# Six loads of keys and values move to a later place in a fused attention and expert kernel

## The chip, the cores and the metric

The kernel runs on one core of a Trainium2 chip. The time is the device time of one execution in microseconds; the figure for a kernel is the median of its runs. A core has TensorE (PE in the profile; its weight loads are PEld), VectorE (DVE), ScalarE (ACT), GpSimd (POOL) and SyncE (SP), and 16 DMA engines that serve the queues on which POOL and SP issue transfers.

## The reference

Keys and values are averaged over groups of 8 positions, softmax attention is done with the queries, and the context goes through four experts, whose outputs are added with per-token weights.

```
B, H, S, D = 8, 8, 576, 64                      # x: (4608, 512); 4 experts, hidden 1024
k_p, v_p = mean of k, v over groups of 8        # 72 pooled positions per head
attn = softmax(q @ k_p.T / sqrt(D)) @ v_p       # per batch and head
x = attn.transpose(0, 2, 1, 3).reshape(B * S, H * D)
for e in range(4):
    out += p[:, e:e + 1] * (relu(x @ w1[e]) @ w2[e])   # p: domain_probs normalised over e
```

## The kernel before

**Tiles and steps.** The 4608 tokens are 36 tiles of 128; four tiles are a group of 512. A batch has 576 tokens, so it covers four and a half tiles. The experts run in 36 steps (9 groups by 4 experts), each of 12 slots. In every three slots TensorE does two up-projections (`up`, L453, four matmuls each, for the next step) and one down-projection (`down`, L486, eight matmuls, for this step). That stream is the frame; all attention work for a later group is put between its slots.

**The plan.** `at(slot, fn, ...)` files a call under a slot, and the last loop emits, for each slot, the expert work first and then the calls filed there. Nothing is reordered afterwards: each engine runs its instructions in the order in which they were emitted. For tile t of groups 2 to 8, `base = (E * g - 5 + i) * SLOTS`, so tile 8 has base 36, tile 9 has 48, and so on by 12. `plan_tile` (L527) puts the scores (`sc`, L320) at slot base, the transposing DMA of the softmax weights (`attnT`, L390, SP) at base + 1, and the context (`x_ps`, L410) at base + 6. Directly behind the context it puts the transposing DMA of `x_sb` into `xT` (L430, SP), a `gate` on POOL and the load of the queries of tile t + 3 (`qrow`, L108, POOL).

**The gate.** `gate(t)` (L525) is a one-element POOL copy that reads `x_sb` of tile t. All that POOL issues behind it, loads included, therefore waits for the context of that tile.

**Keys and values.** A batch's raw keys and values are loaded by POOL with a cast to bf16 into `kraw` and `vraw` (L80 and L84: 512 and 64 KB each), two buffers of each. When a tile t begins a batch that was not prepared yet, `plan_batch` (L519) files, ahead of that tile, `prep_k` (DVE sums and mask, giving `kpad`) at base - 9, `prep_kT` at base - 6 and `prep_v` at base - 5. For batches 2 to 7 `prep_kT` is one transposing DMA on SP, `kT<-kpad` (L259). The first `sc` of the batch needs it at slot base, six slots later. Batch 2 begins with tile 9; batches 3, 4, 5, 6 and 7 are first needed by tiles 13, 18, 22, 27 and 31.

**The loads in question.** `waiting` is a list that starts with the loads of batch 3 and gets those of batch b + 2 when batch b is planned. In each pass over a tile, one load is taken from the list and filed at base + 6, so on POOL it stands behind the gate and the query load of that tile:

```
done_batches, waiting = 2, [(load_k, 3), (load_v, 3)]
...
    plan_tile(t, base - 2, -9 if t > 2 * TPG else 0)
    if waiting:
        load, b = waiting.pop(0)
        at(base + 6, load, b)
```

Slot base + 6 of tile t is slot (base of t + 1) - 6. So where tile t + 1 begins a batch, its `kT<-kpad` is filed at the same slot as a load that the pass over tile t files. In the kernel before this is so for tile 8 (batch 2, slot 42) and for no other tile, since the list is empty in the passes over tiles 12, 17, 21, 26 and 30.

Of the kernel before, what the change touches and what calls it, by code (L numbers as in the profile page):

```python
# [17 lines left out]
def kernel(  # L18
# [12 lines left out]
    B, H, S, D = q.shape  # L31
    E, DM, F = moe_w1.shape
    P = nc.NUM_PARTITIONS
# [481 lines left out]
    def at(slot, fn, *args):  # L515
        plan.setdefault(slot, []).append((fn, args))

    def plan_batch(b, slot):
        at(slot + 5, prep_k, b)  # L519
        at(slot + 8, prep_kT, b)  # L520
        at(slot + 9, prep_v, b)
# [5 lines left out]
    def plan_tile(t, slot, turn=0):  # L527
        exp, norm, move, sum_v = (3, 4, 3, 8) if by_dma(t) else (4, 5, 8, 10)
        at(slot + turn, turn_q, t)
        at(slot + 2, scores, t)  # L530
        at(slot + 2, less_max, t)
        at(slot + exp, expo, t)
        at(slot + move, attn_T, t)
        at(slot + norm, sums if by_dma(t) else normalise, t)
        at(slot + sum_v, context, t)
        if by_dma(t):
            at(slot + sum_v, gate, t)
            if t + 3 < NT:
                at(slot + sum_v, load_q, t + 3)
# [7 lines left out]
    done_batches, waiting = 2, [(load_k, 3), (load_v, 3)]  # L547
    for g in range(2, NG):
        for i in range(TPG):
            t = g * TPG + i  # L550
            base = (E * g - 5 + i) * SLOTS
            last_b = ((t + 1) * P - 1) // S
            if last_b >= done_batches:
                plan_batch(last_b, base - 2 - SLOTS)
                done_batches += 1
                if last_b + 2 < B:
                    waiting += [(load_k, last_b + 2), (load_v, last_b + 2)]
            plan_tile(t, base - 2, -9 if t > 2 * TPG else 0)
            if waiting:
                load, b = waiting.pop(0)  # L560
                at(base + 6, load, b)

# [198 lines left out]
```

## Time and profile before

| | us |
|---|---|
| median of 3 runs | 555.86 |
| lowest and highest of them | 554.24, 556.35 |
| the profiled execution, its own time | 556.4 |
| its span in the profile | 554.4 |
| TensorE busy in the span | 542.0 (98%) |
| `h_ps` L453 and `o_ps` L486 together | 547.5, of which each overlaps the next |
| POOL busy | 70.6 (13%) |

The last row but one is longer than TensorE's whole busy time because matmuls are pipelined: one begins before the one ahead of it has ended. Start times, not the durations of single matmuls, tell how long a stretch takes. "Landing" of a DMA is the time from its issue to the moment its last byte is signalled.

### The profile page before, as it was taken

The page shows a single profiled execution, that of the slowest core. Times are in us where ns is not written, and L with a number is a line of the kernel's source. Part 1 is how long each engine was busy: PE and PEld are TensorE (multiplying, and loading weights), DVE is VectorE, ACT ScalarE, POOL GpSimd, SP SyncE. Part 2 cuts the span into 40 slices and gives each one's busy share as a digit, 9 for nine tenths or more (in the row PEclk, how much of TensorE's full clock was granted, in tenths as well). Part 3 has the DMA queues.
Part 4 walks back from the last instruction along what each step waited for, and adds up shares of the span by engine and source line. Part 5 has one row for each costly group of instructions (what it writes and reads, how often), then busy time and mean ns, then how long its engine had stood idle before and what let it go on. Part 6 is the DMA issues. An engine that isn't in the chain of part 4 may idle for free.

```text
span 554.4 us, 7323 instructions
## 1 busy us (share of the span) xinstructions
PE 542.0 (98%) x2929; PEld 261.3 (47%) x2929; DVE 264.7 (48%) x456; ACT 213.5 (39%) x355; POOL 70.6 (13%) x120
## 2 busy tenths in 40 slices
PE   7899998999999999999999999999999999999997
PEld 3664553444444444444444444444444444444443
DVE  4874846344644445644463444744474444422223
ACT  3554653233333333333333333333333333333330
POOL 7234002111101100112011100101010000000000
PEclk9999999899999999999999999999999999999999
DMA  9999918455745534366535553334333431111002
GB/s 200 206 200 200 199 8 137 74 80 79 122 82 83 84 59 99 53 84 74 116 48 77 84 116 41 52 41 98 60 54 40 74 74 32 21 39 38 1 0 77
DMA packets 110689, 45.84 MB, mean 83 GB/s; under 512 B 87584, under 2 KB 106016, under 8 KB 110656
## 3 DMA queue, kind: packets, MB, share of 16 engines
q0 software_dynamic: 51472, 22.03, 32.3%
q1 hardware_dynamic: 59184, 23.35, 17.8%
q8 instruction: 23, 0.38, 0.3%
q14 instruction: 10, 0.08, 0.0%
HBM read 45.16 MB, written 9.44 MB: 98 GB/s over the span
## 4 chain that ended last, share of the span: by engine, by line
PE 93%; DMA 3%; DVE 2%; ACT 1%; issue 0%; POOL 0%; SPq 0%; POOLq 0%
PE o_ps L486 44%; PE h_ps L453 43%; PE x_ps L410 2%; PE sc L320 2%; DMA kT<-kpad 1%; PE h_ps L469 1%; DMA kraw<-in_k_dram 1%; PE x_ps L436 1%; PE o_ps L571 0%; DVE acc L501 0%; PE at_ps L394 0%; ACT attnT L395 0%; PE qT_ps L310 0%; DVE kraw L235 0%; DVE vraw L235 0%
## 5 line engine op out<-in xcount | busy, mean ns | idle before, releaser
L457 ACT ACTIVATE h_sb<-h_ps 128x512 bf16<-128x512 f32 x280 | 167.2, 597 | 301.3 <-PE h_ps L453 301.1
L453 PE MATMUL h_ps<-xT,w 128*128 128x512 bf16 x1120 | 275.2, 380 | 0.0
L486 PE MATMUL o_ps<-w,h_sb 128*128 128x512 bf16 x1152 | 272.3, 379 | 0.0
L486 PEld LDWEIGHTS <-h_sb 128*128 128x128 bf16 x1152 | 112.5, 98 | 134.5 <-issue 1.1
L501 DVE SCALAR_TENSOR_TENSOR acc<-o_ps,p_sb,acc 128x512 f32<-128x512 f32 x108 | 81.0, 750 | 180.4 <-PE o_ps L486 180.4
L453 PEld LDWEIGHTS <-w 128*128 128x128 bf16 x1120 | 106.1, 98 | 117.2 <-issue 0.6
L497 DVE TENSOR_SCALAR acc<-o_ps,p_sb 128x512 f32<-128x512 f32 x36 | 27.0, 750 | 62.1 <-PE o_ps L486 62.1
L525 POOL COPY gated<-x_sb 1x1 bf16<-1x1 bf16 x28 | 7.8, 278 | 372.2 <-DVE x_sb L416 372.2
L334 DVE TENSOR_REDUCE mx<-sc 128x8 f32<-128x576 f32 x36 | 27.2, 756 | 14.1 <-PE sc L320 14.1
L108 POOL DMA_DIRECT2D qrow<-in_q_dram x36 | 30.5, 850 | 26.3 <-DMA w<-in_moe_w_dram 15.2
L338 DVE TENSOR_TENSOR d_sb<-sc,mx 128x576 f32<-128x576 f32 x36 | 27.3, 757 | 1.2
L416 DVE SCALAR_TENSOR_TENSOR x_sb<-x_ps,rs 128x512 bf16<-128x512 f32 x29 | 20.1, 692 | 12.5 <-PE x_ps L410 12.1
L351 ACT ACTIVATE attn<-d_sb 128x576 bf16<-128x576 f32 x29 | 19.8, 682 | 3.6 <-DVE d_sb L338 0.5
L372 DVE TENSOR_REDUCE es<-attn 128x8 f32<-128x576 bf16 x28 | 20.8, 744 | 0.0
L320 PE MATMUL sc<-kT,qT 128*128 128x144 bf16 (+1 forms) x160 | 15.3, 229 | 3.1 <-DMA kT<-kpad 2.9
L320 PEld LDWEIGHTS <-qT 128*128 128x128 bf16 (+1 forms) x160 | 11.2, 101 | 11.5 <-issue 5.5
L410 PEld LDWEIGHTS <-attnT 128*128 128x128 bf16 (+1 forms) x160 | 12.2, 100 | 7.3 <-issue 1.3
L410 PE MATMUL x_ps<-vbd,attnT 128*128 128x192 bf16 (+5 forms) x160 | 14.7, 231 | 0.0
L571 PE MATMUL o_ps<-still 128*128 128x512 bf16 x38 | 11.8, 436 | 1.3 <-DVE still L144 1.3
L235 DVE TENSOR_TENSOR vraw<-vraw 128x1280 bf16<-128x1280 bf16 (+1 forms) x14 | 9.2, 654 | 0.2
L235 DVE TENSOR_TENSOR kraw<-kraw 128x1280 bf16<-128x1280 bf16 (+1 forms) x14 | 9.0, 640 | 0.2
L469 PE MATMUL h_ps<-xT,w 128*128 128x128 bf16 x128 | 7.8, 219 | 0.7 <-ACT xT L442 0.4
(76 smaller groups left out, 148.9 us busy)
## 6 DMA issues: line engine op xcount, KB each, us to landing
out_dram<-acc SPq DMA_DIRECT2D x36, 256.0 KB, 2.0
vraw<-in_v_dram POOLq DMA_DIRECT2D x8, 512.0 KB, 7.6
w<-in_moe_w_dram POOLq DMA_DIRECT2D x8, 512.0 KB, 16.1
w<-in_moe_w_dram POOLq DMA_DIRECT2D x4, 1024.0 KB, 16.2
kraw<-in_k_dram POOLq DMA_DIRECT2D x7, 512.0 KB, 7.3
qrow<-in_q_dram POOLq DMA_DIRECT2D x28, 128.0 KB, 3.8
qg<-in_q_dram SPq DMA_DIRECT2D x1, 1024.0 KB, 5.7
kraw<-in_k_dram POOLq DMA_DIRECT2D x2, 256.0 KB, 6.7
```

The costliest lines, as they stand in the source:

```text
L108: nc.gpsimd.dma_start(out=qrow[t][at:at + n], in_=q[b][:, tok:tok + n, :].rearrange("h p d -> p h d"),)
L320: nc.tensor.matmul(sc[at:at + n, pair // 2, (pair % 2) * PW:(pair % 2 + 1) * PW], lhsT=qT[t][:, pair, at:at + n], rhs=kT[b][:].rearrange(" ...
L334: nc.vector.reduce_max(out=mxs[t][:], in_=by_head(t), axis=AX.X)
L338: nc.vector.tensor_tensor(out=st[t][:], in0=by_head(t), in1=mxs[t][:].unsqueeze(3).to_broadcast([P, 2, 4, SP]), op=ALU.subtract,)
L372: nc.vector.reduce_sum(out=es[:], in_=e, axis=AX.X)
L410: nc.tensor.matmul(ps[at:at + n, h0 * D:(h0 + c1 - c0) * D], lhsT=attnT[t][:, i, at:at + n], rhs=flat[:, c0 * D:c1 * D], start=(i == 0), s ...
L416: nc.vector.scalar_tensor_tensor(out=x_sb[:].rearrange("p (h d) -> p h d", d=D), in0=ps[:].rearrange("p (h d) -> p h d", d=D), scalar=V_ME ...
L453: nc.tensor.matmul(ps[:], lhsT=w1_sb[e][:, kc, fb * P:(fb + 1) * P], rhs=xT[g][:, kc, :], start=(kc == 0), stop=(kc == KC - 1),)
L457: nc.scalar.activation(out=hs[s][:, fb, :], in_=ps[:], func=ACT.Relu)
L486: nc.tensor.matmul(ps[:], lhsT=hs[s][:, fb, i * P:(i + 1) * P], rhs=w2_sb[e][:, fb, :], start=(fb == 0), stop=(fb == FB - 1),)
L497: nc.vector.tensor_scalar_mul(out=accs[t][:], in0=ps[:], scalar1=p_sb[:, e, t:t + 1])
L501: nc.vector.scalar_tensor_tensor(out=accs[t][:], in0=ps[:], scalar=p_sb[:, e, t:t + 1], in1=accs[t][:], op0=ALU.mult, op1=ALU.add,)
```

## The change

A load is taken from the list only in passes in which the tile after this one begins no batch that is still to be planned. In a pass where it does, the load stays at the head of the list for the next pass.

```
             plan_tile(t, base - 2, -9 if t > 2 * TPG else 0)
-            if waiting:
+
+            if waiting and ((t + 2) * P - 1) // S < done_batches:
                 load, b = waiting.pop(0)
                 at(base + 6, load, b)
```

Worked through for all tiles, this moves six loads and leaves four; the number in each cell is the tile whose gate the load stands behind:

| load | k3 | v3 | k4 | v4 | k5 | v5 | k6 | v6 | k7 | v7 |
|---|---|---|---|---|---|---|---|---|---|---|
| before | 8 | 9 | 10 | 11 | 13 | 14 | 18 | 19 | 22 | 23 |
| after | 9 | 10 | 11 | 13 | 14 | 15 | 18 | 19 | 22 | 23 |

Taken by places: the place behind tile 8 no longer has a load, the place behind tile 15 gets one, and the other places keep one, of keys where it was of values and the other way round. No instruction is added or taken away, and only POOL's order changes; the orders of PE, DVE, ACT and SP are the same.

## The prediction

> **What bounds the kernel now.** I read the busy shares first, then TensorE's waits behind the start-up, the chain of work that ended last, and the order in time around the one wait. The page's shares and its clock row:
>
> ```profile
> PE 542.0 (98%) x2929; PEld 261.3 (47%) x2929; DVE 264.7 (48%) x456; ACT 213.5 (39%) x355; POOL 70.6 (13%) x120
> ...
> PEclk9999999899999999999999999999999999999999
> ```
>
> TensorE is busy for 542.0 of 554.4 us: 12.4 us of idleness is all there is. In the clock row one slice, the eighth (97 to 111 us), is below full speed. Of the list of waits from 60 us to the end, this is the only line in which a PE matmul waited:
>
> ```profile
> PE sc L320 <- DMA kT<-kpad: 2.9, 1, 2.9
> ```
>
> So behind the start-up, which the change doesn't touch, TensorE stands once, for 2.9 us. The chain of waits has the same transfer as its only DMA there:
>
> ```profile
> 89.62 7.65 DMA kT<-kpad
> ```
>
> The order in time around it, four engines of it:
>
> ```profile
> 89.07 0.88 POOL L108 DMA_DIRECT2D qrow<-in_q_dram  x1
> 89.62 1.28 SPq L259 DMA_TRANSPOSE kT<-kpad  x1
> ...
> 89.94 0.76 POOL L80 DMA_DIRECT2D kraw<-in_k_dram  x1
> ...
> 91.45 3.36 SPq L509 DMA_DIRECT2D out_dram<-acc  x2
> ...
> 93.50 1.03 PE L453 MATMUL h_ps<-xT,w 128*128 128x512 bf16 x4
> ...
> 97.41 0.64 PE L320 MATMUL sc<-kT,qT 128*128 128x144 bf16 x4 [2.88 <-DMA kT<-kpad]
> ```
>
> The keys of batch 2 are turned from 89.62 on, the raw keys of batch 3 start to load 0.3 us later, and the turned keys land at 97.27 (89.62 + 7.65). The first scores of tile 9 start at 97.41. Four `h_ps` matmuls stand ahead of them from 93.50; undisturbed, four take 0.86 us (from 112.43 to 113.29 in the next step), so the scores could have begun at 94.36.
>
> **The whole price of the stall** is more than the wait. The stretches of one microsecond (columns: busy of PE, PEld, DVE, ACT, POOL, then the granted clock):
>
> ```profile
> 96.00:97.00 1.00, 0.00 (x0) 0.00 (x0) 0.00 (x0) 0.00 (x0) 0.00 (x0) 1.00 1.18 256
> 97.00:98.00 1.00, 0.59 (x5) 0.61 (x6) 0.00 (x0) 0.00 (x0) 0.00 (x0) 0.53 1.18 270
> 98.00:99.00 1.00, 1.00 (x4) 0.29 (x2) 0.88 (x2) 0.00 (x0) 0.00 (x0) 0.50 0.64 195
> 99.00:100.00 1.00, 1.00 (x4) 0.32 (x3) 0.63 (x1) 0.21 (x1) 0.00 (x0) 0.50 0.04 16
> 100.00:101.00 1.00, 1.00 (x5) 0.46 (x4) 0.00 (x0) 0.96 (x2) 0.00 (x0) 0.77 0.00 0
> ```
>
> The granted clock falls to half at about 97.1 and is back at about 100.5, so the first work after the wait runs at half speed. The price comes from like places in two steps: the run of eight `h_ps` matmuls in the slots 39 and 40 starts at 82.81, that of slots 51 and 52 at 101.74, that of slots 63 and 64 at 116.13. The step with the stall takes 18.93 us, the next one, with the same work, 14.39. The stall costs 4.54: 2.88 of wait and 1.66 of slow clock.
>
> **What goes.** The change takes `load_k(3)` from behind tile 8, so nothing of 576 KB starts beside this transpose. How soon would it land then? The other five `kT<-kpad` of the same trace have no load of keys or values beside them. The answers by window give 4.3, 4.1, 3.7, 4.0 and 4.5 us to landing, against 7.7 here. All five have a query load beside them, as this one keeps (in four it is issued 0.5 to 0.8 us ahead, as here). The one of 4.3, at 151.80, also has two output stores issued 1.83 us behind it, just as here (91.45 - 89.62 = 1.83). So neither explains the 7.7; the raw keys do. By the slowest of the five it lands at 89.62 + 4.5 = 94.12; with 0.14 from landing to the matmul (97.27 to 97.41) the scores can start at 94.26, and TensorE gets to them at 94.36. The wait goes whole, with 0.1 us to spare by the slowest row and 0.5 by the median (4.1). No idle piece is then left to slow the clock. Gain: 4.54, of which I take 4.5.
>
> What is late next? The scores of tile 9 also need `qT` of tile 9, issued at 84.78 with 2.4 us to landing: no. Behind them, the softmax up to the issue of `attnT` takes 2.74 us in an undisturbed tile (113.29 to 116.03), its landing 2.6; the context comes about 7.2 us behind the scores (28 matmuls at 0.216 plus 0.25, then four more): 1.8 us of slack, and no PE wait is listed there for any tile.
>
> **What moves.** Each load costs POOL 0.76 + 0.56 = 1.3 us of issue; POOL then waits 11 to 13 us for the next gate, so nothing queues behind it. SP, the other queue, keeps its order. Costed at nothing, with cover:
>
> - Six loads come later. A step of 12 slots is 14.39 us, a slot 1.2. The tightest are v3, filed at slot 66 and folded at slot 91, and k3, at 54 and 87: 30 and 40 us, against a landing of at most 8.9 for any such load here. Their buffers were read long before (v5 at slot 126 follows the fold of v3 at 91). If this cover went, DVE and the next `kT` would be late; 20 us are in the way.
> - The places behind tiles 9, 10, 11, 13 and 14 have a load before and after, of the same size. Nothing changes there.
> - The place behind tile 15 is new: about 195.8, beside `xT` of tile 15, issued at 194.29. The first matmul of the next group needs it at 199.35, 5.06 us later. Trace rows with a load in the same place: 3.1 (tile 9), 3.3 (tile 10), 2.5 (tile 11), 3.2 (tile 19); without one 2.5. So 1.8 us of slack remain at the worst row. Below nothing isn't possible: no matmul waits there now. From above: stretched as `kT` was (7.65 - 4.1 = 3.55), it lands in 6.05, a wait of 1.0. I take nothing, by the four rows in that very place. `attnT` of tile 16, at 202.96, may meet the end of the load (at most 195.8 + 8.9 = 204.7); the slowest landing of any `attnT` is 3.5, and its context is at 207.37: 0.9 to spare.
>
> **The sum.** The profiled execution took 556.4 (span 554.4, 2.0 around it). 556.4 - 4.54 = 551.9, span 549.9. That execution lies 0.5 above the median of the runs, 555.86; on the median's footing 555.86 - 4.5 = 551.4, which I give.
>
> **A rule against part of it.** The row: the clock fell to half some 2.6 us into an idle piece of 2.9 us. The Trainium skill, "TensorE: Matmul & The Clock Gate", in "The HAM clock gate (the "warmup" mystery)", has the clock fall after at least one idle window of about 3.4 us, from windows that run freely. By that rule a 2.9 us gap should cost its length alone, 556.4 - 2.88 = 553.5; by the row it is 551.9. The same section's 3.4 us until full speed returns agrees with the row's 97.1 to 100.5. I go by the row for this execution. Whether every run pays the 1.66 the trace can't say; the lowest run shown, 554.24, is 1.62 under the median, about that sum, which is an estimate from two rows and no proof.
>
> **Rivals.**
>
> 1. *The transpose is still late, by less.* For: 0.1 us is all that the slowest row leaves. Against: the median row leaves 0.5. At a landing of 6 us, midway between the 4.5 and the 7.65, the wait is 1.4; the clock, which fell 2.6 us into the gap, stays. 551.4 + 1.4 = 552.8. 8%.
> 2. *The change doesn't do what it says:* something else made this transpose slow (it is the first of its kind by this path, and it stands behind the stores of 86.09), so the stall stays: 555.9. Against: the row at 151.80 has the same stores on both sides (147.39 and 153.63) and 4.3. 5%.
> 3. *Slower: the load behind tile 15 holds up `xT` of tile 15* until it is through itself. The place is the first `h_ps` of the next group at 199.35. By the slowest load, 8.9, it would end at 204.7: a wait of 5.3 and a slow clock of 1.66, together 7.0, less the 4.5 gained: 558.4. It decides from a landing of 9.6 us on (5.06 + 4.54), or 7.9 with the slow clock. Against: 2.5 to 3.3 in four rows of this very place. 2%.
>
> **Numbers.** Forecast 551.4 at 85%, rivals 8, 5 and 2. From 554.24 - 4.54 = 549.7, the fastest run with the whole price off, to 556.4 - 2.88 = 553.5, the slowest with the wait alone gone; that takes in the forecast and the first rival, and leaves out 7% and the rare. About 0.5% (2.8 us) is what a measurement of this kernel can tell from no change. Faster by more: the forecast and half of the first rival, taken down a little for runs that never paid the slow clock: 0.87. Within: 0.09. Slower: 0.04, the third rival and what I haven't seen.
>
> **What would show it.** Right: no PE wait on `kT<-kpad` behind the start-up; its landing near 4.1; the clock row at 9 in the eighth slice; 14.4 us from the slots 39 and 40 to 51 and 52; `xT` of tile 15 within 3.3. Wrong: a wait of `h_ps` L453 near 195 us on `xT`, or a landing over 4.7 of this `kT` without the raw keys beside it.

## The result, and the profile after

| | before | after |
|---|---|---|
| median, us (6 runs each) | 555.10 | 551.94 |
| lowest and highest | 554.23, 556.35 | 551.66, 552.01 |
| ratio, 95% interval | | 0.994 (0.9923 to 0.9957) |
| profiled execution, its span | 554.4 | 549.9 |

The kernel is faster by 3.2 us. The six runs after lie within 0.35 us. Those before lie in two groups, three at 554.2 to 554.3 and three at 555.9 to 556.4, and why they do is taken up with the run of that kernel again. Three single executions in the experiments took 665.74, 958.99 and 2564.28 us, far over all others of their kernels, and are left out of every median, ratio and range below.

The page of the changed kernel, its shares and its clock row:

```profile
PE 537.4 (98%) x2873; PEld 260.8 (47%) x2929; DVE 264.7 (48%) x456; ACT 213.5 (39%) x355; POOL 70.7 (13%) x120
...
PEclk9999999999999999999999999999999999999999
```

The eighth slice of the clock row is back at 9. (The trace has 2873 of PE's 2929 matmuls; some records are missing, so PE's busy time isn't compared.) In the list of waits from 60 us on no PE matmul waits for anything any more. The order in time at the same place:

```profile
89.12 0.88 POOL L108 DMA_DIRECT2D qrow<-in_q_dram  x1
89.67 1.28 SPq L259 DMA_TRANSPOSE kT<-kpad  x1
...
91.50 3.36 SPq L509 DMA_DIRECT2D out_dram<-acc  x2
...
93.55 1.03 PE L453 MATMUL h_ps<-xT,w 128*128 128x512 bf16 x4
...
94.41 0.41 PE L320 MATMUL sc<-kT,qT 128*128 128x144 bf16 x4
```

The scores start 0.86 us behind the four up-projections ahead of them, and carry no bracket with a wait. The DMA issues from 88 to 99 us have what was 7.7 before (last column: us to landing):

```profile
kT<-kpad SPq DMA_TRANSPOSE x1, 4.0
```

The step from the slots 39 and 40 (82.86) to 51 and 52 (97.25) takes 14.39 us, as every step does.

### The profile page after: what moved, and what is told of

Read it like the earlier page. It is cut to its first block, busy times and chain, and to the rows that moved or that the text cites. A ratio compares the mean times of both kernels' runs of the same rounds, so it can differ in the third digit from the quotient of the medians.

```text
span 549.9 us, 7267 instructions
## 1 busy us (share of the span) xinstructions
PE 537.4 (98%) x2873; PEld 260.8 (47%) x2929; DVE 264.7 (48%) x456; ACT 213.5 (39%) x355; POOL 70.7 (13%) x120
## 4 chain that ended last, share of the span: by engine, by line
PE 96%; DMA 1%; DVE 1%; issue 1%; ACT 1%; POOL 0%; POOLq 0%
PE o_ps L486 45%; PE h_ps L453 44%; PE x_ps L410 2%; PE sc L320 2%; PE h_ps L469 1%; DMA kraw<-in_k_dram 1%; PE x_ps L436 1%; PE o_ps L572 0%; PE at_ps L394 0%; ACT attnT L395 0%; PE qT_ps L310 0%; POOL kraw L80 0%; DVE mx L334 0%; DVE d_sb L338 0%; DVE acc L501 0%
## 5 line engine op out<-in xcount | busy, mean ns | idle before, releaser
L453 PE MATMUL h_ps<-xT,w 128*128 128x512 bf16 x1088 | 271.8, 379 | 1.5
```

What stands on the lines that cost most here:

```text
L453: nc.tensor.matmul(ps[:], lhsT=w1_sb[e][:, kc, fb * P:(fb + 1) * P], rhs=xT[g][:, kc, :], start=(kc == 0), stop=(kc == KC - 1),)
```

## The experiments

Theory A is that of the prediction: the load of keys beside the transpose is the whole cause. Its rivals are B, that the later places of the other loads bring a part, and, per experiment, that something else at this place makes the transpose slow. Theory C, that a part of the runs doesn't pay the slow clock, is to explain the two groups and with them the 3.2 us in place of 4.5. Theory D came later, from a miss.

The kernels start from the kernel before. Except for that kernel run again and the last experiment, they give the places of the loads outright, in this form; only what differs from it is shown below:

```
-            if waiting:
-                load, b = waiting.pop(0)
+            for load, b in {
+                8: [(load_k, 3)], 9: [(load_v, 3)], 10: [(load_k, 4)], 11: [(load_v, 4)],
+                13: [(load_k, 5)], 14: [(load_v, 5)], ...
+            }.get(t, ()):
                 at(base + 6, load, b)
```

**One move alone.** Only k3 leaves its place.

```
-                8: [(load_k, 3)], 9: [(load_v, 3)],
+                9: [(load_k, 3), (load_v, 3)],
```

> Only the load of k3 is moved, from behind tile 8 to behind tile 9, where it stands ahead of v3; all other loads stay as in the kernel before. Theory A (the load beside the transpose is the whole cause): no PE wait on kT<-kpad, span 549.9, time 551.9 as in the changed kernel. Theory B (part of the gain comes from the later places of the other five loads): between 552.5 and 554. If the doubled load behind tile 9 hurts, xT of tile 9 lands in more than 5 us and a PE wait of up to 1 us stands at the first up-projection of its group; I expect no such wait, since tile 9 is not the last of its group.

551.78 us, ratio 0.9947 (0.9927 to 0.9967). No PE wait behind the start-up, landing 4.1. The whole gain is in this one move. Two loads behind tile 9 cost no time either, though `attnT` of tile 10, issued with 3.5 us of them still to come, lands in 4.2 in place of 2.6; no matmul waits for it.

**The other five moves alone.** k3 stays behind tile 8.

```
-                9: [(load_v, 3)], 10: [(load_k, 4)], 11: [(load_v, 4)], 13: [(load_k, 5)], 14: [(load_v, 5)],
+                10: [(load_v, 3)], 11: [(load_k, 4)], 13: [(load_v, 4)], 14: [(load_k, 5)], 15: [(load_v, 5)],
```

> The load of k3 stays behind tile 8; the other five loads stand where the changed kernel has them. Theory A: nothing is gained, a wait of 2.9 us on kT<-kpad, landing near 7.7, time as before (554.2 to 556.4). Theory B: 1 us or more under the kernel before in runs of the same clock.

Ratio 0.9999 (0.9987 to 1.0012). The wait stays, shorter than I expected: 2.1 us, with a landing of 6.9. Theory B is out: the later places are worth nothing, and cost nothing.

**Values in place of keys.**

```
-                8: [(load_k, 3)], 9: [(load_v, 3)],
+                8: [(load_v, 3)], 9: [(load_k, 3)],
```

> The loads of k3 and v3 change places: values stand behind tile 8, keys behind tile 9. Theory A (it is the traffic, whatever it carries): landing of kT<-kpad of 7 to 8 us, wait of 2.5 to 3.3, time 554 to 556.5. Rival (something about keys, such as the buffer beside the one being folded): landing near 4.2, no wait, time 551.9.

Landing 7.1, wait 2.3 (a little under what I had given it), median 555.92, ratio 1.0019 (1.0006 to 1.0033); seven of its ten runs lie at 555.87 or over. It is the traffic, not what it carries or which buffer it fills.

**The kernel before again, with the clock of each run beside its time.**

> The kernel before, unchanged, run several times so that the granted clock of each run stands beside its time. Theory C (the runs of the kernel before fall into two groups, near 554.3 and 556.1, because the slow clock of 1.66 us is paid in some executions and not in others): runs near 556.1 have a mean granted clock of 0.997, runs near 554.3 one of 0.999 to 1.000, and the groups lie 1.6 to 1.9 apart. Rival (the wait itself has two lengths): the clock is the same in both groups. By theory C the wait alone costs 554.3 - 551.9 = 2.4 and the clock 1.8 on top.

Of its 12 runs, the five from 555.64 to 556.49 all have a mean clock of 0.997; the four lowest, 554.07 to 554.30, have 1.000. Theory C holds for these groups, 1.7 us apart. Of the three runs in between, 554.66 has 1.000, while 554.47 and 554.84 have 0.997 too: in one execution of that kind, the profile of the run with five moves (span 552.7), the clock had fallen between 10 and 15 us, in the start-up, and stayed whole at the stall. So the mean clock alone doesn't say where it fell; I take a fall at the stall only where the time is at 555.6 or over. Its own profiled execution (span 553.6) has a shorter wait than the one the prediction was made from, and the clock falls all the same. Its wait, and its stretches of one microsecond (busy PE, PEld, DVE, ACT, POOL, then the clock):

```profile
PE sc L320 <- DMA kT<-kpad: 2.1, 1, 2.1
```

```profile
95.00:96.00 1.00, 0.00 (x0) 0.00 (x0) 0.00 (x0) 0.02 (x1) 0.00 (x0) 1.00 1.15 214
96.00:97.00 1.00, 0.56 (x6) 0.47 (x7) 0.11 (x1) 0.00 (x0) 0.00 (x0) 1.00 1.14 264
97.00:98.00 1.00, 1.00 (x5) 0.34 (x4) 0.97 (x2) 0.00 (x0) 0.00 (x0) 0.59 0.89 214
98.00:99.00 1.00, 1.00 (x4) 0.35 (x3) 0.44 (x1) 0.85 (x2) 0.00 (x0) 0.50 0.32 107
99.00:100.00 1.00, 1.00 (x3) 0.29 (x2) 0.00 (x0) 0.31 (x1) 0.00 (x0) 0.50 0.00 0
100.00:101.00 1.00, 1.00 (x5) 0.42 (x4) 0.00 (x0) 0.00 (x0) 0.00 (x0) 0.70 0.49 94
```

TensorE is at work again from 96.44, and the clock falls only at about 97.2, behind the gap, for 3.4 us. In the runs with values there and with a second place (below), waits of 2.3 and 2.2 us left it whole, and one of 2.87 further down does too. So between 2.1 and 2.9 us it isn't the length of the gap that decides.

What fits all of these gaps is where they lie in time. In each trace the records of the granted clock begin and change at whole multiples of 3.413 us from one another (in the trace before at 4.90, 97.06, 100.47 and 554.44, in this one at 5.03, 97.19 and 100.60), so I cut each trace into windows of that length. In the three executions with a fall at the gap, one window holds 2.53 us (before), 2.11 (this one) and 2.38 (both loads of batch 3, below) of it, and the clock falls at the end of that window. Of the five gaps over 2 us without a fall, no window holds more than 1.99 (second place sooner, first wait), 1.63 (values there), 1.53 (second place sooner, second wait), 1.41 (five moves) and 1.30 (second place). Eight gaps agree with this reading; no run was made to test it.

**Half the load there.** `load_k_top` loads two of the four full row blocks, `load_k_rest` the others and the tail.

```
-                8: [(load_k, 3)], 9: [(load_v, 3)],
+                8: [(load_k_top, 3)], 9: [(load_k_rest, 3), (load_v, 3)],
```

> Behind tile 8 stand only 256 KB of k3 (two of its four full row blocks); the other 320 KB stand behind tile 9, ahead of v3. Theory A with sharing (the transpose gets a part of each DMA engine as long as the load runs): the load is over earlier, kT<-kpad lands in 5 to 6.5 us, a wait of 0.4 to 1.9, time 552.2 to 553.8. Theory C (the clock falls only where the idle piece is long enough): at such a wait the clock never falls, so no run of this kernel lies 1.7 above the others for it. Rival (any load beside it costs the same, as a fixed price for switching between queues): landing near 7, wait over 2.

552.71 us, ratio 0.9958 (0.9946 to 0.997). Landing 5.2, wait 0.4. The wait goes with the bytes, and no run stands 1.7 above the rest (nine runs, 552.59 to 553.44). That the clock never falls is not shown: the two slowest, 553.29 and 553.44, have mean clocks of 0.996 and 0.995, and no profile tells where it fell in them.

**A second transpose with a load behind it.**

```
-                13: [(load_k, 5)],
+                12: [(load_k, 5)],
```

> The kernel before with the load of k5 moved from behind tile 13 to behind tile 12, so that a second transpose, that of the keys of batch 3, has a load beside it. Theory A: two waits on kT<-kpad, the second of 1.5 to 2.9 us (the load is issued 0.8 us behind this transpose where it is 0.3 for the first), landing of the second 6.3 to 7.7 where it was 4.3; time 556 to 560. Rival (only the first transpose of its kind is slow): one wait, time as before, 553.8 to 556.1.

Theory A as I held it falls here: no second wait, 554.46 us, ratio 0.9999 (0.9985 to 1.0014). The order in time around the second transpose, and its line in the list of issues from 148 to 158 us (last column: us to landing):

```profile
149.53 1.27 SPq L259 DMA_TRANSPOSE kT<-kpad  x1
...
150.37 0.76 POOL L80 DMA_DIRECT2D kraw<-in_k_dram  x1
...
154.30 0.45 PE L320 MATMUL sc<-kT,qT 128*64 128x144 bf16 x8
```

```profile
kT<-kpad SPq DMA_TRANSPOSE x1, 4.3
```

The load, which takes 8.5 us to land, runs beside it until it is in, and yet the transpose lands in 4.3. The difference to the first place is half a microsecond: this load is issued 0.84 us behind its transpose, that of k3 0.32. From this came theory D: what counts is whether POOL is through with issuing the load (0.84 + 0.76 = 1.6 us behind the start of the transpose here, 0.32 + 0.76 = 1.1 at the first place) before SP is through with issuing the transpose (1.3).

**The load at the old place, but after the landing.** POOL reads an element of the turned keys first.

```
+    def gate_keys(b):
+        nc.gpsimd.tensor_copy(out=gated[:], in_=kT[b][0:1, 0, 0:1])
...
+                if t == 8:
+                    at(base + 7, gate_keys, 2)
+                    at(base + 7, load, b)
```

> The kernel before, but POOL reads one element of the turned keys of batch 2 ahead of the load of k3, so that this load keeps its place behind tile 8 and starts only once the transpose has landed. Theory A: landing near 4.1, no wait, 551.7 to 552.0, as the changed kernel. Rival (POOL's or the buffer's work at this place, not the two transfers at one time, is the cause): a wait of 2 us or more stays.

Half right. The transpose lands in 4.0 and nothing waits for it, but the time is 553.66, ratio 0.9983 (0.9968 to 0.9999), for a new wait stands behind it:

```profile
PE x_ps L410 <- DMA attnT<-attn: 1.6, 1, 1.6
```

The line of that transpose in the list of issues from 85 to 100 us:

```profile
attnT<-attn SPq DMA_TRANSPOSE x1, 6.2
```

The load, now issued at 94.48, meets the next transpose, that of the softmax weights of tile 9, issued at 97.37; this lands in 6.2 us where the median is 2.6. So a transpose issued into a running load can be stretched too, not that of the keys alone. It depends on how much of the load is still to come. Here it was 5.4 us of the load's 7.9. In the traces of all these kernels an `attnT` issued with at most 1.8 us of a load to come lands in 2.6 as a rule (3.7 at the most).

**Both loads of batch 3 there.**

```
-                8: [(load_k, 3)], 9: [(load_v, 3)],
+                8: [(load_k, 3), (load_v, 3)],
```

> Both loads of batch 3, keys and values, stand behind tile 8 (1.15 MB in place of 0.58); none stands behind tile 9. Sharing (the transpose runs beside the load and gets a part of the engines): the first load lasts longer than the transpose already, so the second changes little: landing 6.9 to 8, wait 2.1 to 3.3, time 553.8 to 557. Rival (the transpose waits until what was queued ahead of it or beside it is through): landing over 10 us, wait over 5, time over 557.

Landing 7.2, wait 2.4, ratio 1.0003 (0.9988 to 1.0019). Twice the bytes queued change nothing, so the transpose doesn't wait until all of them are through. (The second load stands behind the first on POOL's queue; what more traffic at one and the same time would do, this run doesn't show.) Nor does it wait for the first load: it lands at 96.9, that load at 98.8, and in the trace before at 97.27 and 98.8. So the two run side by side. The Trainium skill says how in "DMA: Bandwidth & Descriptors", "Queues, rings and completion order": each DMA engine takes turns, packet by packet, between the queues that have work. These landings, 7.2 against 6.9 to 7.7 with one load, agree; that taking turns is what stretches the transpose no run shows.

**The small part first.** A second version of the load, used for k3 alone, issues its two parts in the other order, so that the 512 KB part is issued 0.85 us behind the transpose.

```
+    def load_k_tail_first(b):
...
+        nc.gpsimd.dma_start(out=kraw[b % 2][0:TAIL, NB - 1, :], in_=rows[(NB - 1) * P:ROWS])
+        nc.gpsimd.dma_start(
+            out=kraw[b % 2][:, 0:NB - 1, :],
...
-                8: [(load_k, 3)],
+                8: [(load_k_tail_first, 3)],
```

> The kernel before, with the two parts of the load of k3 behind tile 8 issued the other way round: the 64 KB part first, then the 512 KB part. The large part is so issued about 0.9 us behind the transpose in place of 0.3 us; same place, same bytes. Theory D, formed from the run with a second place (there the load was issued 0.84 us behind its transpose, which landed in 4.3 us with no wait): what decides is whether the large load is issued before SP has finished issuing the transpose (1.3 us) or behind; here the large load's issue ends at about 1.65 us behind the start of the transpose, in the kernel before at 1.1. Landing 4 to 5, wait under 0.5, time 551.8 to 552.5; a wait on attnT of up to 1 us may stand in its place, since the load ends later. Theory A as first held (any load in flight beside the transpose): landing near 7, wait over 2, 553.8 to 556.

552.47 us, ratio 0.9948 (0.9932 to 0.9964): for theory D. Landing 5.2 (0.2 over what I had given it), wait 0.4, no wait on `attnT`. Same place, same bytes, half a microsecond of order: most of the gain. The order in time:

```profile
89.70 1.28 SPq L267 DMA_TRANSPOSE kT<-kpad  x1
...
90.02 0.55 POOL L94 DMA_DIRECT2D kraw<-in_k_dram  x1
...
90.55 0.79 POOL L95 DMA_DIRECT2D kraw<-in_k_dram  x1
...
95.05 0.41 PE L328 MATMUL sc<-kT,qT 128*128 128x144 bf16 x4 [0.45 <-DMA kT<-kpad]
```

**The second place, sooner.** As with the second place, but the load stands ahead of the query load on POOL.

```
+                if t == 12:
+                    plan[base + 6].insert(-1, (load, (b,)))
```

> As the run with the second place, but behind tile 12 the load of k5 stands ahead of the query load of tile 15, so that it is issued about 0.1 us before the transpose of the keys of batch 3 in place of 0.84 us behind it. Theory D: the second stall now comes: landing 6.5 to 7.7, wait on kT<-kpad of 1.5 to 3 us, two waits in all, time 555.8 to 560. Rival (only the first such transpose, or batch 2, is slow): landing near 4.3, one wait, 553.7 to 556.

559.08 us, ratio 1.006 (1.0036 to 1.0083), and two waits, 5.0 us together. The second one:

```profile
149.58 0.78 POOL L80 DMA_DIRECT2D kraw<-in_k_dram  x1 [0.36 <-issue]
149.71 1.28 SPq L259 DMA_TRANSPOSE kT<-kpad  x1
...
157.79 0.41 PE L320 MATMUL sc<-kT,qT 128*64 128x144 bf16 x4 [2.87 <-DMA kT<-kpad]
```

It lands in 8.0, where the same place gave 4.3. (The query load, ahead of the transpose there, is now 1.2 us behind it; at the first place the query load is ahead and the transpose slow all the same.) In this execution the clock stayed whole at both waits (1.000, span 555.6). The five runs also show the price of the clock three times over: 557.41 and 557.61 with a mean clock of 1.000, 559.08 and 559.15 with 0.997, 560.53 with 0.994: by their clocks no, one and two falls, some 1.5 us each, if they fell at the waits; of these runs only that of 557.61 was profiled.

**The transpose sooner.** The load stays; batch 2 is prepared three slots ahead.

```
-                plan_batch(last_b, base - 2 - SLOTS)
+                plan_batch(last_b, base - 2 - SLOTS - (3 if last_b == 2 else 0))
```

> The kernel before with the load of k3 left behind tile 8, and the preparation of batch 2 filed three slots (3.6 us) earlier, so that the transpose is issued at about 86 us and the load starts some 4 us behind it. Theory D: landing 4 to 4.6, no wait, 551.7 to 552.2. It then falls to a second question: is xT of tile 8 or another transpose stretched by the load in a way that TensorE notices? I expect not, as xT of tile 8 is issued 1.2 us ahead of the load. Rival (the stretch has nothing to do with the load): landing near 7 and, with 3.6 us more to spare, still no wait: the landing time tells the two apart, not the time of the run.

552.54 us, ratio 0.9945 (0.9924 to 0.9965). Issued at 86.88, it lands in 2.6, the shortest of all. But `attnT` of tile 9, issued at 97.26 beside the end of a load that came 1.2 us later, takes 5.0, and TensorE waits 0.4 for it. That load then had 3.5 us still to come. My guess that TensorE would notice nothing was wrong by that 0.4, and so were the landing of 4 to 4.6 and the 551.7 to 552.2 that I had given it.

No version is faster than the changed kernel by more than the noise (the lowest median is 551.78, with k3 alone moved): TensorE has no wait left behind the start-up that a moved load could take away.

## Why the prediction was right, and where it was off

- **The stall goes whole: right.** Landing 4.0 against a bound of 4.5, the scores at 94.41 against 94.36, no wait.
- **Its cause: right in kind, too coarse in rule.** The raw keys do it, by the run with k3 alone. But "a load beside it" isn't enough: the second place has one and lands in 4.3. What decides is the order of issue within half a microsecond: landings of 6.9 to 8.0 with the 512 KB load issued between 0.13 us ahead and 0.33 behind, 4.3 at 0.84 behind, and 5.2 at 0.85 behind with the 64 KB part 0.32 behind. I had read the other five transposes only for having no load beside them.
- **What moves costs nothing: right.** By the run with the other five moves, 0.9999. In the profile after, `xT` of tile 15, issued at 189.81 with a load 1.5 us behind it, lands in 2.5, and its first matmul at 194.87 doesn't wait. That isn't owed to each execution: in the other runs seven `xT` with a load 1.5 us behind them land in 3.9 to 4.5, though no matmul waits for one.
- **The bound for `attnT` was too kind.** I took 3.5 as its slowest landing. In those rows no load was running, or one with at most 0.9 us to come; with 3.5 us to come it takes up to 5.0, with 5.4 us 6.2. In the changed kernel this is harmless: no `attnT` is issued with more than 1.4 us of a load to come, and the slowest beside one lands in 3.6.
- **The sum: right for the profiled execution, off by 0.5 for the median.** Span 549.9 and time 551.9 were given, and 549.9 and 551.91 came. The step that was off is the move to "the median's footing": 555.86 - 4.5 = 551.4, against 551.94. It takes both terms as if each run paid them in full. The wait of 2.88 was a long one (profiles with 576 KB or more at the same place show 2.1 to 2.4), and the 1.66 of slow clock is paid in a part of the runs: those at 555.6 and over, 3 of the 6 shown above, 5 of 12 in the run again. By the windows of 3.41 us an estimate for a gap of 2.1 is (3.41 - 2.1) / 3.41 = 38% of the runs, those in which it lies whole in one window. The lower group of the six lies 2.3 above the changed kernel, about what a wait of 2.1 to 2.4 costs alone. Beside the experiments the kernel before had medians of 554.54, 554.71 and 555.39, as this part changed. A stall whose slow clock comes and goes is worth, between the medians of the result, 3.2 us, not 4.5. What doesn't vary is the time once it is gone, 551.66 to 552.01, and that was to be had from the profiled execution's own time.
- **The clock rule.** I weighed the trace's fall after a gap of 2.9 us against the Trainium skill, "TensorE: Matmul & The Clock Gate", "The HAM clock gate (the "warmup" mystery)", which wants at least one idle window of 3.4 us. The runs decide against the length: the clock falls after gaps of 2.11, 2.38 and 2.88. They agree with two other points there: the windows run freely (the traces' windows of 3.413 us, which the gaps don't shift), and the slow stretch lasts 3.4 us. What the traces add is that a window need not be idle throughout: 2.11 us of it went with a fall, 1.99 did not.
- **The third rival** didn't come at tile 15, but its mechanism is real: it is what the load after the landing met at `attnT`, which came in at 103.5, some 0.7 us behind the end of the load.

## What to carry to other kernels

When a small transfer that is needed soon is slow in one place, compare the order of issue with a place where it is quick, down to tenths of a microsecond; a large load that goes out half a microsecond later may leave it alone. Read the price of a stall from like places a step apart, since the clock's part of it lies behind the wait. Subtract that price from the execution that shows it, not from a median over runs that may not have paid it.

## What the runs showed of the hardware

- A transposing DMA of keys issued up to 0.13 us behind, or up to 0.33 us ahead of, a 512 KB load on the other queue lands in 6.9 to 8.0 us, 0.33 ahead of 256 KB in 5.2, 0.84 ahead of 512 KB in 4.3, and with only a query load close by in 3.7 to 4.5 (once 5.0). Why half a microsecond decides was not measured; that SP's 1.3 us of issue must be over before the load's packets come is a conjecture that these kernels agree with and none proves.
- The transposing DMA of softmax weights, issued into a running load, is stretched by what is still to come of it: 2.6 us to landing as a rule with up to 1.8 us to come, 4.2 and 5.0 with 3.5, 6.2 with 5.4.
- The granted clock changes only at the ends of windows of 3.413 us, which a gap of TensorE doesn't shift. In these eight gaps it fell where 2.11 us or more lay within one window, at that window's end, and not where 1.99 or less did. So it can fall about 0.7 us after work has begun again (96.44 to 97.2), on account of a gap that is already over.
